# Head sums and weight spreading of a windowed attention on TensorE, with score and value steps as two streams

## The chip, the cores and the metric

One core of a Trainium2 chip. The metric is the device time of one execution, in microseconds, lower is better. Each kernel ran in alternating rounds with the kernel before, on the same chip. There were four such batches: the result, e1 to e4, e5 to e8 (both of these on chip 15), and e9 (on chip 13). Where two variants of different batches are compared, the kernel before is the link: its medians in the four batches are 1617.2, 1617.2, 1617.2 and 1617.1 us. Times of one kernel agree within about 0.2%.

Engine names as the profile writes them: PE is TensorE's matmul stream, PEld its weight loads, DVE is VectorE, ACT is ScalarE, POOL is GpSimd, SP is the engine that issues most DMAs.

## The reference

Two layers, each an attention block and a gated feed-forward block, on 2048 tokens of width 1024, bf16. Cut to what matters:

```python
def _A_ref(x, wqkv, wo):                 # 32 heads of 32 lanes
    W, dil = 8, 2                        # each token looks at itself and 7 tokens before it, 2 apart
    ...                                  # q, k, v = x @ wqkv; kg, vg = k, v at those 8 places
    logits = jnp.einsum("bhsd,bhswd->bhsw", q, kg) * scale
    logits = jnp.where(mask[None, None, :, :], logits, -1e9)
    attn = _softmax(logits, axis=-1)
    o = jnp.einsum("bhsw,bhswd->bhsd", attn, vg)
    ...                                  # @ wo

def _B_ref(x, w1, w3, w2): ...           # silu(x@w1) * (x@w3) @ w2, inner width 3584

x = x + _A_ref(_layernorm(x), ...);  x = x + _B_ref(_layernorm(x), ...)     # twice
```

The projections and the feed-forward are large matmuls. The scores and the weighted sum of values are elementwise products with short sums, because each token has its own eight keys.

## The kernel before

The program itself decides the order of the instructions on each engine: it keeps a clock of its own (`now`) for PE, VectorE and ScalarE, advances it by an expected cost for each instruction it emits, and fits attention steps into VectorE's gaps (`background`). PE and VectorE then execute strictly in that order.

The attention works on 16 pieces of 256 tokens ("halves"). Lanes are laid out so that each of the 128 partitions holds 8 of the 1024 lanes, and four neighbouring partitions make one head. So the sum over a head is a sum over 8 tiles in the same partition, which VectorE does as a tree, and then over 4 partitions, which it does with a 32x32-block transpose (arguments shortened):

```python
xnp = ctx.enter_context(tc.tile_pool(name="xn", bufs=4))     # normalised rows, waiting for their transpose
scr = ctx.enter_context(tc.tile_pool(name="scr", bufs=2))    # products of the trees
# ... cut ...
def apply(i):                                                # in norm_apply
    xn = xnp.tile([P, D], BF16, name="xn")
    nc.vector.tensor_scalar(xn[:], x_sb[:, c * TPC + j, :], mv[:, i, 0:1], rstd[:, i:i + 1], ...)
    nc.sync.dma_start_transpose(out=xnT[:, :, j * P:(j + 1) * P], in_=xn[:])
# ... cut ...
def attention_steps():
    for g, (l, h) in enumerate(halves):
        # ... cut: psm = products q*k, summed by a tree over the 8 tiles
        yield 2.35, 0.0, lambda: V.transpose(psmT, psm)           # 128x2048
        yield 2.35, 0.0, lambda: V.reduce_sum(L, psmT, axis=AX.X) # sum over 4 partitions
        # ... cut: max by three steps, subtract, exp on ScalarE, sum by three steps, reciprocal, multiply: An
        yield 1.25, 0.0, lambda: V.tensor_copy(AeT, An repeated 4 times)
        yield 2.35, 0.0, lambda: V.transpose(At, AeT)             # weights back on every lane
        # ... cut: oT = products At*v, summed by a tree
```

The output projection of a half (`o_tile`, 16 matmuls for 128 tokens, twice for a half) is placed in PE's order when the program's clock says that `oT` is ready.

Of the kernel before, what the change touches and what calls it, by code (L numbers as in the profile page):

```python
# [9 lines left out]
ALU = mybir.AluOpType  # L10
# [5 lines left out]
def kernel(  # L16
# [46 lines left out]
    PSUM, DRAM = bass.MemoryType.PSUM, bass.MemoryType.DRAM  # L63
    const = ctx.enter_context(tc.tile_pool(name="const", bufs=1))
    wp = ctx.enter_context(tc.tile_pool(name="wp", bufs=8))
    xnp = ctx.enter_context(tc.tile_pool(name="xn", bufs=4))
    xtp = ctx.enter_context(tc.tile_pool(name="xnT", bufs=2))
    scr = ctx.enter_context(tc.tile_pool(name="scr", bufs=2))
    wk = ctx.enter_context(tc.tile_pool(name="wk", bufs=1))
    smp = ctx.enter_context(tc.tile_pool(name="smp", bufs=1))  # L70
    sgp = ctx.enter_context(tc.tile_pool(name="sg", bufs=3))
# [10 lines left out]
    MM, TABLE, DMA = 0.216, 1.3, 2.5  # L82
    now = dict(pe=23.6, dve=15.0, act=24.5, table=None)
    units = [(l, c) for l in range(2) for c in range(NCH)]
    norms, attention = [], []
    x_at = [12.5, 21.5, 25.0, 28.5]
    xnT_at, norm_left, qkv_at, oT_at, o_todo = {}, {}, {}, {}, {}

# [37 lines left out]
    def background(until):  # L126

        while True:
            for queue in (norms, attention):
                s = head(queue)  # L130
                if s is not None and max(now["dve"], s[1]) + s[0] <= until:
                    take(queue)
                    break
            else:
                return
# [8 lines left out]
    def bank(name):  # L144
# [3 lines left out]
    nc.gpsimd.memset(ident[:], 0.0)  # L148
    nc.gpsimd.affine_select(out=ident[:], in_=ident[:], compare_op=ALU.not_equal, fill=1.0, base=0,
                            pattern=[[-1, P]], channel_multiplier=1)  # L150
    maskT = const.tile([P, W, 8], FP32, name="maskT")
    nc.gpsimd.memset(maskT[:], 0.0)
    for a in range(4):
        mslice = maskT[32 * a:32 * (a + 1), :, :]
        nc.gpsimd.affine_select(out=mslice, in_=mslice, compare_op=ALU.is_ge, fill=-1.0e9, base=0,
                                pattern=[[-DIL, W], [0, 8]], channel_multiplier=1)
    epst = const.tile([P, 1], FP32, name="epst")
    nc.gpsimd.memset(epst[:], EPS)

# [235 lines left out]
        qks[l, h] = qT, kT, max(now["dve"], qkv_at[l, h // R, 1]) + DMA  # L395

    def load_v(l, h):
        if (l, h) in vs or (l, h // R, 2) not in qkv_at:
            return
        vT = qkvp.tile([P, KT, HALO + TCH], BF16, name="vT")  # L400
        load_part(vT, l, 2, h * TCH, True)
        vs[l, h] = vT, max(now["dve"], qkv_at[l, h // R, 2]) + DMA

    def attention_steps():

        halves = [(l, h) for l in range(2) for h in range(NCH * R)]
        V = nc.vector
        for g, (l, h) in enumerate(halves):
            load_qk(l, h)
            while (l, h) not in qks:  # L410
                yield "blocked"
                load_qk(l, h)
            load_v(l, h)
            qT, kT, ready = qks[l, h]
            psm = wk.tile([P, W, TCH], BF16, name="psm")

            def mul_qk(w_):
                pr = scr.tile([P, KT, TCH], BF16, name="pr", tag="scr")
                k0 = HALO - DIL * w_
                V.tensor_tensor(pr[:], qT[:], kT[:, :, k0:k0 + TCH], op=ALU.mult)  # L420
                return pr

            yield 0.0, ready, lambda: None
            yield from tree(W, mul_qk, lambda w_: psm[:, w_, :])
            load_v(l, h)
            NE = TCH // 32 * 8
            psmT = smp.tile([P, W * NE, 4], BF16, name="psmT", tag="tr")
            L = smp.tile([P, W, NE], FP32, name="L", tag="L")
            m4 = smp.tile([P, 4, NE], FP32, name="m4", tag="m4")
            mx = smp.tile([P, NE], FP32, name="mx")  # L430
            E = smp.tile([P, W, NE], BF16, name="E")
            sm_ = smp.tile([P, NE], FP32, name="sm_")
            rs = smp.tile([P, NE], FP32, name="rs")
            rsb = smp.tile([P, NE], BF16, name="rsb")
            at = {}

            def exps():
                V.tensor_tensor(L[:], L[:], mx[:].unsqueeze(1).to_broadcast([P, W, NE]), op=ALU.subtract)
                nc.scalar.activation(E[:], L[:], ACTF.Exp, scale=scale)
                at["E"] = act(0.65, now["dve"] + 0.1, "exp")  # L440

            yield 2.35, 0.0, lambda: V.transpose(psmT[:].rearrange("p c d -> p (c d)"),  # L442
                                                 psm[:].rearrange("p w s -> p (w s)"))
            yield 2.35, 0.0, lambda: V.reduce_sum(L[:].rearrange("p w e -> p (w e)"), psmT[:], axis=AX.X)
            if h == 0:
                yield 0.2, 0.0, lambda: V.tensor_tensor(L[:, :, 0:8], L[:, :, 0:8], maskT[:], op=ALU.add)
            yield 0.46, 0.0, lambda: V.tensor_tensor(m4[:], L[:, 0:4, :], L[:, 4:8, :], op=ALU.max)
            yield 0.33, 0.0, lambda: V.tensor_tensor(m4[:, 0:2, :], m4[:, 0:2, :], m4[:, 2:4, :], op=ALU.max)
            yield 0.26, 0.0, lambda: V.tensor_tensor(mx[:], m4[:, 0, :], m4[:, 1, :], op=ALU.max)
            yield 0.72, 0.0, exps  # L450
            e4 = smp.tile([P, 4, NE], FP32, name="e4", tag="m4")
            An = smp.tile([P, W, NE], BF16, name="An", tag="L")
            yield 0.46, at["E"], lambda: V.tensor_tensor(e4[:], E[:, 0:4, :], E[:, 4:8, :], op=ALU.add)
            yield 0.33, 0.0, lambda: V.tensor_tensor(e4[:, 0:2, :], e4[:, 0:2, :], e4[:, 2:4, :], op=ALU.add)
            yield 0.26, 0.0, lambda: V.tensor_tensor(sm_[:], e4[:, 0, :], e4[:, 1, :], op=ALU.add)
            yield 0.60, 0.0, lambda: V.reciprocal(rs[:], sm_[:])
            yield 0.23, 0.0, lambda: V.tensor_copy(rsb[:], rs[:])
            yield 0.46, 0.0, lambda: V.tensor_tensor(An[:], E[:], rsb[:].unsqueeze(1).to_broadcast([P, W, NE]),
                                                     op=ALU.mult)
            AeT = smp.tile([P, W * NE, 4], BF16, name="AeT", tag="tr")  # L460
            At = wk.tile([P, W, TCH], BF16, name="At")
            yield 1.25, 0.0, lambda: V.tensor_copy(
                AeT[:], An[:].rearrange("p w e -> p (w e)").unsqueeze(2).to_broadcast([P, W * NE, 4]))
            yield 2.35, 0.0, lambda: V.transpose(At[:].rearrange("p w s -> p (w s)"),
                                                AeT[:].rearrange("p c d -> p (c d)"))
            if g + 1 < len(halves):
                load_qk(*halves[g + 1])
            load_v(l, h)
            while (l, h) not in vs or (g >= 2 and o_todo.get(halves[g - 2], 1)):
                yield "blocked"  # L470
                load_v(l, h)
            vT, ready = vs[l, h]
            oT = wk.tile([P, KT, TCH], BF16, name="oT", bufs=2)
            oTs[l, h] = oT

            def mul_v(t):
                tm = scr.tile([P, W, TCH], BF16, name="tm", tag="scr")
                base = vT[:, t, HALO:HALO + TCH]
                win = bass.AP(vT.tensor, base.offset, [list(base.ap[0]), [-DIL, W], [1, TCH]])
                V.tensor_tensor(tm[:], At[:], win, op=ALU.mult)  # L480
                return tm

            yield 0.0, ready, lambda: None
            yield from tree(KT, mul_v, lambda t: oT[:, t, :])
            oT_at[l, h] = now["dve"]
            o_todo[l, h] = 2

    oTs = {}
    attention.append([attention_steps(), None])

    NW = 8
    seq = [("qkv", which, h) for which in range(3) for h in range(2)]
# [46 lines left out]
    def o_tile():  # L539

        l, n = o_queue.pop(0)
        h, j = n // 2, n % 2
        force(attention, lambda: (l, h) in oT_at)
        oT = oTs[l, h]
        for hh in range(2):
            ps = bank("po")
            for t in range(KT):
                nc.tensor.matmul(ps[:], lhsT=oT[:, t, j * P:(j + 1) * P], rhs=wo[:, t, hh * 512:(hh + 1) * 512],  # L548
                                 start=(t == 0), stop=(t == KT - 1))
            r = pe(KT, oT_at[l, h] + 0.2)  # L550
            xs = x_sb[:, n, hh * 512:(hh + 1) * 512]
            background(r)
            nc.vector.tensor_tensor(xs, xs, ps[:], op=ALU.add)  # L553
            dve(0.64, r)
        o_todo[l, h] -= 1
        if j == 1:
            norm_queue.append((("B", l, n // TPC), n // TPC, (h % R,)))

    def between(hold, must=False):

        flush()
        while o_queue and (must or oT_at.get((o_queue[0][0], o_queue[0][1] // 2), 1e9) + 0.3 <= now["pe"]):
            o_tile()
            if not must:
                break
        while norm_queue and not hold:
            queue_norm(*norm_queue.pop(0))
# [181 lines left out]
```

## Time and profile before

| | before |
|---|---|
| time, median of 2 runs | 1617.2 us (1616.86 to 1617.55) |
| PE busy | 1601.8 us, 99% of the profiled span |
| VectorE busy | 1164.2 us, 72% |
| ScalarE busy | 353.2 us, 22% |
| PE waits found, in all | 2.9 us, all before 10 us |

From the page of the kernel before: the busy time of each engine with its share of the span, and, further down, the chain of waits that ended last, by engine.

```profile
PE 1601.8 (99%) x7525; PEld 805.9 (50%) x7672; DVE 1164.2 (72%) x1964; ACT 353.2 (22%) x549; POOL 1.9 (0%) x12
...
PE 94%; DVE 3%; DMA 1%; issue 1%; SPq 0%; ACT 0%; DVEq 0%
```

PE is busy nearly all the time, and the chain lies on PE. But a busy PE is not yet PE at its peak, so two more views are wanted. First the list of PE's waits (engine, line and tile that waited, who released it: us in total, times, the longest).

```profile
PE pw L168 <- DVE psm L163: 1.2, 1, 1.2
PE pT L277 <- DVE xn L268: 1.0, 1, 1.0
PE pq L286 <- DMA wqkv<-in_A_wqkv_dram: 0.7, 1, 0.7
```

Then the table by stage: length, busy time (and records) of PE, PEld, DVE, ACT, POOL, then the granted TensorE clock, the DMA share and GB/s.

```profile
40.00:100.00 60.00, 59.68 (x274) 39.88 (x279) 53.16 (x90) 21.40 (x39) 0.00 (x0) 1.00 0.52 145
100.00:200.00 100.00, 99.53 (x456) 61.32 (x464) 96.83 (x163) 32.14 (x55) 0.00 (x0) 1.00 0.72 213
```

464 weight loads in the 100 us of the second stage, one for each matmul, is one matmul of 512 columns every 216 ns, at a clock of 1.00. (Some matmul records are missing, so the loads are the better count.) The Trainium skill, "TensorE: Matmul & The Clock Gate", Part 1, section "Wait — 56ns, not 53.3ns?", has 215.7 ns measured for this size, from start to start, and the trace agrees. So the stream has no slack: whatever is added to PE must lengthen the kernel, and what is taken off VectorE can't shorten it.

The VectorE operations that the change removes, from the groups by shape (line, engine, operation, tiles, shapes, count | busy us, mean ns | idle before):

```profile
L442 DVE STREAM_TRANSPOSE psmT<-psm 128x2048 bf16<-128x2048 bf16 x16 | 36.9, 2307 | 0.2
L464 DVE STREAM_TRANSPOSE At<-AeT 128x2048 bf16<-128x2048 bf16 x16 | 36.9, 2306 | 0.1
L444 DVE TENSOR_REDUCE L<-psmT 128x512 f32<-128x2048 bf16 x16 | 36.4, 2276 | 0.1
L462 DVE COPY AeT<-An 128x2048 bf16<-128x2048 bf16 x16 | 19.6, 1225 | 0.4
```

One more view of the kernel before, which the prediction did not look at closely enough: VectorE in order of time (start, length, operation, and in brackets the idle time before it with what ended it), near the beginning.

```profile
26.62 1.00 DVE L211 TENSOR_SCALAR xn<-x_sb,mv,rstd 128x1024 bf16<-128x1024 bf16 x2
...
27.81 1.00 DVE L211 TENSOR_SCALAR xn<-x_sb,mv,rstd 128x1024 bf16<-128x1024 bf16 x2
28.73 1.28 DVE L187 BATCH_NORM_STATS2 st<-x_sb 128x6 f32<-128x512 bf16 x2
...
46.04 1.23 DVE L420 TENSOR_TENSOR pr<-qT,kT 128x2048 bf16<-128x2048 bf16 x1 [6.04 <-DMA qT<-qkv_d]
```

Four normalised tiles are written within 2.2 us, each into a buffer of its own; then VectorE goes on. It even has 6 us to spare before the first product of the scores.

### The profile page before, as it was taken

How to read it: one execution, taken by the hardware profiler on the slowest of the kernel's cores; microseconds unless marked ns; L12 is line 12 of the kernel's file. 1: busy time of each engine (PE TensorE's matmuls, PEld its weight loads, DVE VectorE, ACT ScalarE, POOL GpSimd, SP SyncE). 2: the span in 40 equal slices, each digit the busy share in tenths (PEclk: the TensorE clock that was granted, in tenths of full speed). 3: DMA queues.
4: the chain of work that ended last, by engine and by line, in shares of the span. 5: the costliest groups of instructions: out<-in, count | busy, mean ns of one | idle time of the engine just before them, and what ended most of it. 6: DMA issues, size and time to landing. Idle time of an engine off the chain costs nothing.

```text
span 1615.4 us, 19241 instructions
## 1 busy us (share of the span) xinstructions
PE 1601.8 (99%) x7525; PEld 805.9 (50%) x7672; DVE 1164.2 (72%) x1964; ACT 353.2 (22%) x549; POOL 1.9 (0%) x12
## 2 busy tenths in 40 slices
PE   9999999999999999999999999999999999999999
PEld 7665544444445544455444554445544444444444
DVE  6899998989889898997998349983599832222212
ACT  4332321212112330222302123021230212011110
POOL 0000000000000000000000000000000000000000
PEclk9999999999999999999999999999999999999999
DMA  9565955466538864478663776528675265436430
GB/s 315 138 191 164 262 166 178 131 194 182 174 105 235 249 190 145 137 211 246 159 190 121 210 236 174 190 95 262 207 223 158 94 194 169 144 109 217 156 130 27
DMA packets 336397, 285.84 MB, mean 177 GB/s; under 512 B 69681, under 2 KB 318897, under 8 KB 336177
## 3 DMA queue, kind: packets, MB, share of 16 engines
q1 hardware_dynamic: 336160, 284.46, 58.1%
q8 instruction: 60, 0.98, 0.2%
q14 instruction: 33, 0.26, 0.0%
q10 hardware_dynamic: 144, 0.13, 0.0%
HBM read 239.47 MB, written 29.36 MB: 166 GB/s over the span
## 4 chain that ended last, share of the span: by engine, by line
PE 94%; DVE 3%; DMA 1%; issue 1%; SPq 0%; ACT 0%; DVEq 0%
PE acc L653 24%; PE pu L637 23%; PE pg L629 22%; PE ps L587 19%; PE po L548 6%; PE pq L286 1%; DMA kT<-qkv_d 1%; DMA wqkv<-in_A_wqkv_dram 1%; DVE pr L420 1%; DVE pr L354 0%; DVE hT L641 0%; DVE x_sb L553 0%; DVE st L187 0%; DVE tm L354 0%; DVE tm L480 0%
## 5 line engine op out<-in xcount | busy, mean ns | idle before, releaser
L637 PE MATMUL pu<-xnT,w3t 128*128 128x512 bf16 x1763 | 420.5, 379 | 1.6
L629 PE MATMUL pg<-xnT,w1t 128*128 128x512 bf16 x1750 | 419.5, 379 | 2.1
L653 PE MATMUL acc<-w2t,hT 128*128 128x512 bf16 (+1 forms) x1768 | 387.4, 378 | 1.8
L587 PE MATMUL ps<-xnT,wqkv 128*128 128x512 bf16 x1441 | 317.6, 379 | 1.6
L633 ACT ACTIVATE sg<-pg 128x512 bf16<-128x512 f32 x224 | 133.6, 597 | 779.6 <-PE pg L629 738.9
L641 DVE TENSOR_TENSOR hT<-sg,pu 128x512 bf16<-128x512 bf16 x224 | 152.7, 682 | 191.9 <-PE pu L637 179.1
L653 PEld LDWEIGHTS <-hT 128*128 128x128 bf16 x1804 | 176.5, 98 | 210.5
L637 PEld LDWEIGHTS <-w3t 128*128 128x128 bf16 x1792 | 175.4, 98 | 211.4
L629 PEld LDWEIGHTS <-w1t 128*128 128x128 bf16 x1792 | 175.3, 98 | 211.4
L587 PEld LDWEIGHTS <-wqkv 128*128 128x128 bf16 x1472 | 211.1, 143 | 106.8
L420 DVE TENSOR_TENSOR pr<-qT,kT 128x2048 bf16<-128x2048 bf16 x128 | 155.8, 1218 | 99.5 <-DMA kT<-qkv_d 93.5
L663 DVE TENSOR_TENSOR x_sb<-x_sb,acc 128x512 bf16<-128x512 bf16 x129 | 87.3, 677 | 114.3 <-PE acc L653 109.7
L480 DVE TENSOR_TENSOR tm<-At,vT 128x2048 bf16<-128x2048 bf16 x128 | 156.0, 1219 | 0.2
L591 ACT CAST sgt<-ps 128x512 bf16<-128x512 f32 x184 | 105.1, 587 | 225.1 <-PE ps L587 183.5
L354 DVE TENSOR_TENSOR tm<-tm 128x1024 bf16<-128x1024 bf16 (+1 forms) x256 | 137.1, 552 | 0.5
L354 DVE TENSOR_TENSOR pr<-pr 128x1024 bf16<-128x1024 bf16 (+1 forms) x256 | 137.0, 551 | 0.5
L548 PE MATMUL po<-wo,oT 128*128 128x512 bf16 x503 | 115.3, 379 | 0.6
L548 PEld LDWEIGHTS <-oT 128*128 128x128 bf16 x512 | 50.1, 98 | 60.1
L187 DVE BATCH_NORM_STATS2 st<-x_sb 128x6 f32<-128x512 bf16 x120 | 75.7, 668 | 5.8 <-DMA x_sb<-in_A_x_dram 5.8
L633 ACT ACT_TABLE_LOAD x30 | 38.5, 1283 | 76.9 <-PE pg L629 76.6
L553 DVE TENSOR_TENSOR x_sb<-x_sb,po 128x512 bf16<-128x512 bf16 x64 | 43.1, 683 | 16.3 <-PE po L548 15.9
L442 DVE STREAM_TRANSPOSE psmT<-psm 128x2048 bf16<-128x2048 bf16 x16 | 36.9, 2307 | 0.2
(83 smaller groups left out, 403.7 us busy)
## 6 DMA issues: line engine op xcount, KB each, us to landing
w1t<-in_B_w_dram SPq DMA_DIRECT2D x56, 1024.0 KB, 5.5
w3t<-in_B_w_dram SPq DMA_DIRECT2D x56, 1024.0 KB, 7.8
w2t<-in_B_w_dram SPq DMA_DIRECT2D x48, 1024.0 KB, 5.7
wqkv<-in_A_wqkv_dram SPq DMA_DIRECT2D x28, 1024.0 KB, 6.8
qkv_d<-sgt SPq DMA_DIRECT2D x92, 256.0 KB, 3.3
qT<-qkv_d SPq DMA_DIRECT2D x16, 512.0 KB, 8.6
w2t<-in_B_w_dram SPq DMA_DIRECT2D x16, 512.0 KB, 5.2
kT<-qkv_d SPq DMA_DIRECT2D x14, 544.0 KB, 9.4
```

The source lines that it names most:

```text
L354: nc.vector.tensor_tensor(b[:, 0:m, :], b[:, 0:m, :], b[:, m:2 * m, :], op=ALU.add)
L420: V.tensor_tensor(pr[:], qT[:], kT[:, :, k0:k0 + TCH], op=ALU.mult)
L480: V.tensor_tensor(tm[:], At[:], win, op=ALU.mult)
L548: nc.tensor.matmul(ps[:], lhsT=oT[:, t, j * P:(j + 1) * P], rhs=wo[:, t, hh * 512:(hh + 1) * 512], start=(t == 0), stop=(t == KT - 1))
L587: nc.tensor.matmul(ps[:], lhsT=ws[kk // KH][:, kk % KH, t::KT], rhs=xnT[:, kk, :], start=(kk == 0), stop=(kk == KT - 1))
L591: nc.scalar.copy(sgt[:, t - t0, :], ps[:])
L629: nc.tensor.matmul(pg[:], lhsT=w1t[:, kk, fi * P:(fi + 1) * P], rhs=xnT[:, kk, :], start=(kk == 0), stop=(kk == KT - 1))
L633: nc.scalar.activation(sg[:], pg[:], ACTF.Silu)
L637: nc.tensor.matmul(pu[:], lhsT=w3t[:, kk, fi * P:(fi + 1) * P], rhs=xnT[:, kk, :], start=(kk == 0), stop=(kk == KT - 1))
L641: nc.vector.tensor_tensor(hT[:, f - f0, :], sg[:], pu[:], op=ALU.mult)
L653: nc.tensor.matmul(acc[:], lhsT=hT[:, f - f0, j * P:(j + 1) * P], rhs=w2ts[(f - f0) // 8][:, (f - f0) % 8, q0:q0 + step], start=(f == f0), ...
L663: nc.vector.tensor_tensor(xs, xs, acc[:], op=ALU.add)
```

## The change

The intent: take the transposes, the sum over four partitions and the fourfold copy off VectorE. The sum over the four partitions of a head becomes a matmul with a 0/1 matrix `gather` (128 by 32), one for each quarter of the tokens, put on its own 32 output partitions. The spread of the weights back over the lanes becomes a matmul with a 0/1 matrix `spread` (128 by 128), copied out of PSUM by ScalarE. The generator of attention steps is cut into two, scores and values, so that one can go on while the other waits for PE. Requests for PE are queued and emitted between groups of matmuls, one at a time, when the program's clock says that the input is there. To make room, one `xn` buffer is given for a third `scr` buffer.

```diff
-    xnp = ctx.enter_context(tc.tile_pool(name="xn", bufs=4))
+    xnp = ctx.enter_context(tc.tile_pool(name="xn", bufs=3))
-    scr = ctx.enter_context(tc.tile_pool(name="scr", bufs=2))
+    scr = ctx.enter_context(tc.tile_pool(name="scr", bufs=3))
@@ background @@
-            for queue in (norms, attention):
+            for queue in (norms, values, scores):
@@ constants: gather and spread are built on GpSimd; cut @@
+    def pe_requests(limit=1, must=False):
+        while pe_queue and limit and (must or pe_queue[0][0] + 0.3 <= now["pe"]):
+            pe_queue.pop(0)[1]()
+            limit -= 1
@@ score_steps, after the tree @@
-            yield 2.35, 0.0, lambda: V.transpose(psmT..., psm...)
-            yield 2.35, 0.0, lambda: V.reduce_sum(L..., psmT[:], axis=AX.X)
+            def gather_heads(t):
+                at["L"] = L = psum.tile([P, W, BLK], FP32, name="L", tag="mm")
+                for a in range(4):
+                    nc.tensor.matmul(L[32 * a:32 * (a + 1), :, :], lhsT=gather[:],
+                                     rhs=psm[:, :, a * BLK:(a + 1) * BLK], start=True, stop=True)
+                at["t"] = pe(3, t) + 0.2
+            t = now["dve"] + 0.2
+            pe_queue.append((t, lambda: gather_heads(t)))
@@ max and sum: one tensor_reduce each in place of three steps each; cut @@
-            yield 1.25, 0.0, lambda: V.tensor_copy(AeT..., An... 4 times)
-            yield 2.35, 0.0, lambda: V.transpose(At..., AeT...)
+            def spread_heads(a):
+                ps = psum.tile([P, W, BLK], FP32, name="pe", tag="mm")
+                nc.tensor.matmul(ps[:], lhsT=spread[:, a, :], rhs=An[:], start=True, stop=True)
+                r = pe(1, t2)
+                nc.scalar.copy(At[:, :, a * BLK:(a + 1) * BLK], ps[:])
@@ value_steps: the tree of the values as before, in a generator of its own; cut @@
@@ between: called after each group of matmuls @@
         flush()
+        pe_requests()
```

More of the change, by code (lines that the diff above doesn't have):

```diff
@@ L84 @@
     units = [(l, c) for l in range(2) for c in range(NCH)]
-    norms, attention = [], []
+    norms = []
     x_at = [12.5, 21.5, 25.0, 28.5]
@@ L150 @@
                             pattern=[[-1, P]], channel_multiplier=1)
-    maskT = const.tile([P, W, 8], FP32, name="maskT")
+    maskT = const.tile([32, W, HALO], FP32, name="maskT")
     nc.gpsimd.memset(maskT[:], 0.0)
-    for a in range(4):
-        mslice = maskT[32 * a:32 * (a + 1), :, :]
-        nc.gpsimd.affine_select(out=mslice, in_=mslice, compare_op=ALU.is_ge, fill=-1.0e9, base=0,
-                                pattern=[[-DIL, W], [0, 8]], channel_multiplier=1)
+    nc.gpsimd.affine_select(out=maskT[:], in_=maskT[:], compare_op=ALU.is_ge, fill=-1.0e9, base=0,
+                            pattern=[[-DIL, W], [1, HALO]], channel_multiplier=0)
+    gather = const.tile([P, 32], BF16, name="gather")
+    spread = const.tile([P, 4, P], BF16, name="spread")
+    for t, pattern, base, slope in ((gather, [[-4, 32]], 0, 1), (spread, [[P, 4], [1, P]], 0, -4)):
+        nc.gpsimd.memset(t[:], 1.0)
+        nc.gpsimd.affine_select(out=t[:], in_=t[:], compare_op=ALU.is_ge, fill=0.0, base=base,
+                                pattern=pattern, channel_multiplier=slope)
+        nc.gpsimd.affine_select(out=t[:], in_=t[:], compare_op=ALU.is_ge, fill=0.0, base=3 - base,
+                                pattern=[[-st, n] for st, n in pattern], channel_multiplier=-slope)
     epst = const.tile([P, 1], FP32, name="epst")
@@ L397, in load_v @@
     def load_v(l, h):
-        if (l, h) in vs or (l, h // R, 2) not in qkv_at:
+        if (l, h) in vs or (l, h // R, 2) not in qkv_at or len(av_done) < len(vs):
             return
@@ L402, in load_v, with score_steps @@
         vs[l, h] = vT, max(now["dve"], qkv_at[l, h // R, 2]) + DMA
-    def attention_steps():
-        halves = [(l, h) for l in range(2) for h in range(NCH * R)]
+    pe_queue = []
+    L_at, At_at, Ats, av_done = {}, {}, {}, set()
+    halves = [(l, h) for l in range(2) for h in range(NCH * R)]
+    BLK = TCH // 4
+    def pe_requests(limit=1, must=False):
+        while pe_queue and limit and (must or pe_queue[0][0] + 0.3 <= now["pe"]):
+            pe_queue.pop(0)[1]()
+            limit -= 1
+    def score_steps():
         V = nc.vector
@@ L425, in attention_steps @@
             load_v(l, h)
-            NE = TCH // 32 * 8
-            psmT = smp.tile([P, W * NE, 4], BF16, name="psmT", tag="tr")
-            L = smp.tile([P, W, NE], FP32, name="L", tag="L")
-            m4 = smp.tile([P, 4, NE], FP32, name="m4", tag="m4")
-            mx = smp.tile([P, NE], FP32, name="mx")
-            E = smp.tile([P, W, NE], BF16, name="E")
-            sm_ = smp.tile([P, NE], FP32, name="sm_")
-            rs = smp.tile([P, NE], FP32, name="rs")
-            rsb = smp.tile([P, NE], BF16, name="rsb")
@@ L435, in attention_steps @@
-            at = {}
-            def exps():
-                V.tensor_tensor(L[:], L[:], mx[:].unsqueeze(1).to_broadcast([P, W, NE]), op=ALU.subtract)
-                nc.scalar.activation(E[:], L[:], ACTF.Exp, scale=scale)
-                at["E"] = act(0.65, now["dve"] + 0.1, "exp")
-            yield 2.35, 0.0, lambda: V.transpose(psmT[:].rearrange("p c d -> p (c d)"),
-                                                 psm[:].rearrange("p w s -> p (w s)"))
-            yield 2.35, 0.0, lambda: V.reduce_sum(L[:].rearrange("p w e -> p (w e)"), psmT[:], axis=AX.X)
@@ L445, in attention_steps @@
-            if h == 0:
-                yield 0.2, 0.0, lambda: V.tensor_tensor(L[:, :, 0:8], L[:, :, 0:8], maskT[:], op=ALU.add)
-            yield 0.46, 0.0, lambda: V.tensor_tensor(m4[:], L[:, 0:4, :], L[:, 4:8, :], op=ALU.max)
-            yield 0.33, 0.0, lambda: V.tensor_tensor(m4[:, 0:2, :], m4[:, 0:2, :], m4[:, 2:4, :], op=ALU.max)
-            yield 0.26, 0.0, lambda: V.tensor_tensor(mx[:], m4[:, 0, :], m4[:, 1, :], op=ALU.max)
-            yield 0.72, 0.0, exps
-            e4 = smp.tile([P, 4, NE], FP32, name="e4", tag="m4")
@@ L452, in attention_steps @@
-            An = smp.tile([P, W, NE], BF16, name="An", tag="L")
-            yield 0.46, at["E"], lambda: V.tensor_tensor(e4[:], E[:, 0:4, :], E[:, 4:8, :], op=ALU.add)
-            yield 0.33, 0.0, lambda: V.tensor_tensor(e4[:, 0:2, :], e4[:, 0:2, :], e4[:, 2:4, :], op=ALU.add)
-            yield 0.26, 0.0, lambda: V.tensor_tensor(sm_[:], e4[:, 0, :], e4[:, 1, :], op=ALU.add)
-            yield 0.60, 0.0, lambda: V.reciprocal(rs[:], sm_[:])
-            yield 0.23, 0.0, lambda: V.tensor_copy(rsb[:], rs[:])
@@ L458, in attention_steps @@
-            yield 0.46, 0.0, lambda: V.tensor_tensor(An[:], E[:], rsb[:].unsqueeze(1).to_broadcast([P, W, NE]),
-                                                     op=ALU.mult)
-            AeT = smp.tile([P, W * NE, 4], BF16, name="AeT", tag="tr")
-            At = wk.tile([P, W, TCH], BF16, name="At")
-            yield 1.25, 0.0, lambda: V.tensor_copy(
-                AeT[:], An[:].rearrange("p w e -> p (w e)").unsqueeze(2).to_broadcast([P, W * NE, 4]))
-            yield 2.35, 0.0, lambda: V.transpose(At[:].rearrange("p w s -> p (w s)"),
-                                                AeT[:].rearrange("p c d -> p (c d)"))
@@ L466, in attention_steps @@
             if g + 1 < len(halves):
                 load_qk(*halves[g + 1])
+            at = {}
+            def gather_heads(t):
[5 more added lines that the diff above has]
+            t = now["dve"] + 0.2
@@ new lines, in score_steps @@
+            pe_queue.append((t, lambda: gather_heads(t)))
+            while "t" not in at:
+                yield "blocked"
+            L = at["L"]
+            Ls = smp.tile([P, W, BLK], FP32, name="Ls")
+            mx = smp.tile([P, BLK], FP32, name="mx")
+            E = smp.tile([P, W, BLK], BF16, name="E")
+            sm_ = smp.tile([P, BLK], FP32, name="sm_")
+            rs = smp.tile([P, BLK], FP32, name="rs")
+            An = smp.tile([P, W, BLK], BF16, name="An")
+            yield 0.0, at["t"], lambda: None
@@ new lines, in score_steps, with exps @@
+            if h == 0:
+                yield 0.2, 0.0, lambda: V.tensor_tensor(L[0:32, :, 0:HALO], L[0:32, :, 0:HALO], maskT[:],
+                                                        op=ALU.add)
+            yield 0.68, 0.0, lambda: V.tensor_reduce(mx[:], L[:].rearrange("p w e -> p e w"), op=ALU.max, axis=AX.X)
+            def exps():
+                V.tensor_tensor(Ls[:], L[:], mx[:].unsqueeze(1).to_broadcast([P, W, BLK]), op=ALU.subtract)
+                nc.scalar.activation(E[:], Ls[:], ACTF.Exp, scale=scale)
+                at["E"] = act(0.65, now["dve"] + 0.1, "exp")
@@ new lines, in score_steps @@
+            yield 0.70, 0.0, exps
+            yield 0.0, at["E"] if "E" in at else 0.0, lambda: None
+            yield 0.66, at["E"], lambda: V.tensor_reduce(sm_[:], E[:].rearrange("p w e -> p e w"), op=ALU.add,
+                                                         axis=AX.X)
+            yield 0.56, 0.0, lambda: V.reciprocal(rs[:], sm_[:])
+            yield 0.68, 0.0, lambda: V.tensor_tensor(An[:], E[:], rs[:].unsqueeze(1).to_broadcast([P, W, BLK]),
+                                                     op=ALU.mult)
@@ new lines, in score_steps @@
+            while g >= 1 and halves[g - 1] not in av_done:
+                yield "blocked"
+            At = Ats[l, h] = wk.tile([P, W, TCH], BF16, name="At")
+            t2 = now["dve"] + 0.2
+            def spread_heads(a):
[3 more added lines that the diff above has]
+                nc.scalar.copy(At[:, :, a * BLK:(a + 1) * BLK], ps[:])
+                done = act(0.6, r)
+                if a == 3:
+                    At_at[l, h] = done
@@ L468, in attention_steps, with value_steps @@
+            for a in range(4):
+                pe_queue.append((t2, lambda a=a: spread_heads(a)))
+            while (l, h) not in At_at:
+                yield "blocked"
+    def value_steps():
+        V = nc.vector
+        for g, (l, h) in enumerate(halves):
+            while (l, h) not in At_at or (g >= 2 and o_todo.get(halves[g - 2], 1)):
+                yield "blocked"
             load_v(l, h)
-            while (l, h) not in vs or (g >= 2 and o_todo.get(halves[g - 2], 1)):
+            while (l, h) not in vs:
@@ L470, in attention_steps @@
                 yield "blocked"
                 load_v(l, h)
+            At = Ats[l, h]
             vT, ready = vs[l, h]
@@ L481, in mul_v @@
                 return tm
-            yield 0.0, ready, lambda: None
+            yield 0.0, max(ready, At_at[l, h]), lambda: None
             yield from tree(KT, mul_v, lambda t: oT[:, t, :])
@@ L486, in attention_steps @@
             o_todo[l, h] = 2
+            av_done.add((l, h))
+            if g + 1 < len(halves):
+                load_v(*halves[g + 1])
     oTs = {}
-    attention.append([attention_steps(), None])
+    values, scores = [[value_steps(), None]], [[score_steps(), None]]
     NW = 8
@@ L542, in o_tile @@
         h, j = n // 2, n % 2
-        force(attention, lambda: (l, h) in oT_at)
+        while (l, h) not in oT_at:
+            for queue in (values, scores):
+                if head(queue) is not None:
+                    take(queue)
+                    break
+            else:
+                assert pe_queue
+                pe_requests(1, True)
         oT = oTs[l, h]
```

## The prediction

> **What bounds the kernel now.** TensorE. The page's busy table gives PE 1601.8 us of a 1615.4 us span (99%), the chain that ended last is 94% PE, the granted clock is 1.00. The table by stage shows 99.5 us of PE in every 100 us from 100 to 1600 us, with 463 to 464 weight loads: one 128x512 matmul per 216 ns. (The groups' "mean 379 ns" includes latency that the next matmul overlaps.) The list of PE's waits holds three entries, 2.9 us together, all in the first 10 us. The Trainium skill ("TensorE: Matmul & The Clock Gate", Back-to-back issue gap; measured 215.7 ns for N=512) agrees with this trace: the stream has no idle time to win.
>
> VectorE is 72% busy (1164 us), but PE never waits for it after the start: it is off the critical path.
>
> **What the change removes.** Per half-chunk of attention (16 in all), from the groups by shape: two 128x2048 stream transposes (2.31 us each), the sum over four (2.28), the fourfold copy (1.22), the small max and sum ladders, subtract, reciprocal, casts: about 190 us of VectorE in all.
>
> **What it adds.** VectorE: five operations per half of 0.55 to 0.7 us, some 53 us; so 1164 falls to about 1030 us. ScalarE: 64 evictions at 0.59 us, so 353 rises to about 391. TensorE, in the built order: exactly 128 more matmuls and weight loads, nothing else:
> - 64 spread matmuls, full array, 512 columns: 64 x 0.216 = 13.8 us.
> - 64 gather matmuls of 32 output columns, in 16 groups of four. The skill (same page, Part 3) says matmuls on different 32-column strips run side by side (2.38x for three). Then four cost about 0.3 us, and entering and leaving should expose the neighbours' latency, 379 - 216 = 0.16 us an end: about 0.65 us a group, 10 us in all (estimate). One after another they would take 0.86 + 0.3 us a group, 19 us.
>
> **What moves.** Values come ahead of scores in VectorE's background; gathers and spreads are slipped between PE groups when the program expects their inputs ready. In the built order each projection stands over 100 matmuls (24 us) behind the last spread of its half, so I expect no long wait: 0 to 4 us in total over 32 hand-overs. One scratch buffer more and one xn buffer fewer do nothing; the longer setup on GpSimd costs under 0.5 us.
>
> **Sum.** All PE additions are on the critical path, all VectorE savings off it: 1617 + 13.8 + 10 + 1 = 1642 us, 1.5% slower. Range 1635 to 1650. Faster by over 2%: 1%. Within 2%: 87%. Slower by over 2%: 12%.
>
> **What would show each step.** PE still 99% busy with no idle in the middle, its busy time up by the same 20 to 30 us as the span; spread matmuls spaced by 216 ns; a gather group taking about 0.65 us between its neighbours; VectorE near 1030 us and ScalarE near 391 without effect; PE's waits on VectorE's products and weights under 4 us.
>
> **What would make it wrong.** (a) Gathers serialise, or draining costs more than 0.16 us an end: toward 1650 or above. (b) Inputs of gathers and spreads come later than the program expects, so that PE, in order, stalls a microsecond at each of 32 places: 1650 to 1675. (c) ScalarE, waiting in order for a spread, holds back a gate activation until PSUM buffers run out: PE idle released by ScalarE. (d) Gathers overlap fully: 1635.

## The result, and the profile after

| | before | after |
|---|---|---|
| time, median of 2 runs | 1617.2 us | 1666.4 us |
| ratio after/before | | 1.030 (95% interval 1.027 to 1.033) |
| PE busy | 1601.8 us | 1631.1 us |
| VectorE busy | 1164.2 us | 1042.5 us |
| ScalarE busy | 353.2 us | 387.7 us |
| mean granted clock | 1.000 | 0.993 |

A ratio is the mean time of one kernel's fast runs over that of the other's of the same rounds, so it is not quite the ratio of the medians quoted. The changed kernel is 49.2 us slower, outside the predicted range of 1635 to 1650 us.

The page of the changed kernel, busy times and chain:

```profile
PE 1631.1 (98%) x7650; PEld 813.6 (49%) x7800; DVE 1042.5 (63%) x1820; ACT 387.7 (23%) x611; POOL 3.2 (0%) x15
...
PE 91%; DVE 5%; DMA 3%; issue 1%; SPq 0%; ACT 0%; DVEq 0%
```

There are 128 weight loads more, as predicted, and VectorE lost its 122 us. But 3% of the chain now lies on DMA and 5% on VectorE. PE's waits show it:

```profile
PE L L449 <- DVE psm L362: 9.2, 3, 6.8
PE L L449 <- DVE vT L389: 7.0, 1, 7.0
PE pe L489 <- DVE An L480: 4.3, 2, 4.0
```

20.5 us of PE stalls, 17.8 of them three long ones: two before a gather and one before a spread. (The matmul of the line put down to `vT` reads `psm`, whose last piece was written just before, from 68.47 to 68.76 us.) The table by stage says where, and shows a second effect: the clock.

```profile
40.00:100.00 60.00, 48.82 (x202) 29.09 (x205) 36.75 (x71) 21.90 (x43) 0.00 (x0) 0.86 0.44 124
100.00:200.00 100.00, 92.76 (x417) 58.01 (x424) 70.09 (x125) 31.52 (x54) 0.00 (x0) 0.97 0.58 165
```

Between 40 and 200 us PE lost about 18 us of busy time, and worked at 0.86 and 0.97 of its clock. PE in order of time:

```profile
68.91 0.62 PE L449 MATMUL L<-psm,gather 128*32 128x512 bf16 x4 [6.97 <-DVE vT L389]
69.46 9.52 PE L638 MATMUL ps<-xnT,wqkv 128*128 128x512 bf16 x31
82.98 0.59 PE L489 MATMUL pe<-An,spread 128*128 128x512 bf16 x1 [4.00 <-DVE An L480]
83.36 5.94 PE L638 MATMUL ps<-xnT,wqkv 128*128 128x512 bf16 x16
...
145.12 0.62 PE L449 MATMUL L<-psm,gather 128*32 128x512 bf16 x4 [6.82 <-DVE psm L362]
145.67 8.97 PE L638 MATMUL ps<-xnT,wqkv 128*128 128x512 bf16 x32
...
1062.94 27.79 PE L704 MATMUL acc<-w2t,hT 128*128 128x512 bf16 x126
1090.66 0.40 PE L449 MATMUL L<-psm,gather 128*32 128x512 bf16 x4
1091.00 1.90 PE L680 MATMUL pg<-xnT,w1t 128*128 128x512 bf16 x8
```

After each stall the matmuls are slow for a while: the 32 after the first gather (one record is missing) take 9.5 us, where 31 x 0.216 us and the 0.38 us of the last one, 7.1 us, would do; the next 16, from 83.36 to the next spread at 89.14, take 5.8 us in place of 3.5; the 32 after the second late gather take 8.8 us, up to the spread at 154.48, in place of 6.9. Together 2.4 + 2.3 + 1.9 = 6.6 us. (The first 2.4 us are hidden: at full clock PE would only have waited longer for the spread's input.) The Trainium skill, "TensorE: Matmul & The Clock Gate", Part 1, says that the clock is halved when PE has been idle for a window of about 3.4 us, and comes back after a busy window. For these stalls this trace agrees: the granted clock is 0.50 from 69 to 74 us and from 83 to 88 us, and 1.00 again after. (Shorter stalls are in the list at the end.)

The last three lines are an undisturbed gather. From the start of the last full matmul before it to the first gather are 309 ns in the trace's own time stamps, from there to the next full matmul 332 ns; nearly all undisturbed groups of this kernel and of e5 agree within 2 ns. Without gathers it would be 216 ns from one full matmul to the next. So four gathers cost PE 309 + 332 - 216 = 425 ns, 0.43 us, less than the predicted 0.65 us. (Some expectations below use 0.44, a first reading of this place.)

Why is VectorE late? VectorE in order of time:

```profile
27.36 1.00 DVE L217 TENSOR_SCALAR xn<-x_sb,mv,rstd 128x1024 bf16<-128x1024 bf16 x2
...
28.55 0.55 DVE L217 TENSOR_SCALAR xn<-x_sb,mv,rstd 128x1024 bf16<-128x1024 bf16 x1
38.62 0.55 DVE L217 TENSOR_SCALAR xn<-x_sb,mv,rstd 128x1024 bf16<-128x1024 bf16 x1 [9.52 <-DMA xnT<-xn]
...
50.27 1.18 DVE L436 TENSOR_TENSOR pr<-qT,kT 128x2048 bf16<-128x2048 bf16 x1
...
80.06 0.55 DVE L217 TENSOR_SCALAR xn<-x_sb,mv,rstd 128x1024 bf16<-128x1024 bf16 x1 [6.88 <-DMA xnT<-xn]
```

There are three `xn` buffers, and a chunk has four tiles. The fourth must wait until the transposing DMA of the first has read its buffer: 9.5 us. At this time the DMAs are full (two weight tiles of 1 MB were queued just before; the DMA share between 20 and 40 us is 1.01), and that transpose lands 8.9 us after its issue, where the median is 3.5 us. VectorE executes in order, so everything after it waits too. The first product of the scores starts at 50.27 us, 4.2 us later than before. The same wait comes again at 73 to 80 us (6.9 us) and at 126 to 134 us (8.0 us), each time between VectorE's steps that a gather or spread depends on, and each time PE stalls behind it. The wait at 126 us is like the first (8.3 us from issue to landing). The one at 73 us is not: there the transposes land 3.2 to 3.4 us after their issue, but SP, which issues in order too, comes to the first of them only at 76.66 us, 4.6 us after its rows were written. Before it stands a store that waits for ScalarE's copy of a late output of PE. So the second wait is in part an effect of PE's first stall.

The sum of what the trace shows: spreads 64 x 0.216 = 13.8 us, gathers 16 x 0.425 = 6.8 us, the three long stalls 17.8 us, slow matmuls 6.6 us, later stalls 2.7 us: 48 of 49 us. Whether the stalls come from the `xn` buffer or from the hand-overs themselves is a matter of experiment.

### The profile page after: what moved, and what is told of

It is laid out like the page before. It is cut to its first block, busy times and chain, and to the rows that moved or that the text cites. A ratio compares the mean times of both kernels' runs of the same rounds, so it can differ in the third digit from the quotient of the medians.

```text
span 1664.7 us, 19422 instructions
## 1 busy us (share of the span) xinstructions
PE 1631.1 (98%) x7650; PEld 813.6 (49%) x7800; DVE 1042.5 (63%) x1820; ACT 387.7 (23%) x611; POOL 3.2 (0%) x15
## 4 chain that ended last, share of the span: by engine, by line
PE 91%; DVE 5%; DMA 3%; issue 1%; SPq 0%; ACT 0%; DVEq 0%
PE acc L704 23%; PE pu L688 23%; PE pg L680 22%; PE ps L638 16%; PE po L598 6%; DVE pr L436 1%; DMA xnT<-xn 1%; DVE pr L360 1%; DMA x_sb<-in_A_x_dram 1%; DVE st L193 1%; PE pe L489 1%; DMA kT<-qkv_d 1%; PE L L449 0%; DVE x_sb L603 0%; DVE psm L362 0%
## 5 line engine op out<-in xcount | busy, mean ns | idle before, releaser
L638 PE MATMUL ps<-xnT,wqkv 128*128 128x512 bf16 x1442 | 327.2, 385 | 1.6
L491 ACT CAST At<-pe 128x512 bf16<-128x512 f32 x64 | 37.4, 587 | 75.6 <-PE pe L489 75.6
L217 DVE TENSOR_SCALAR xn<-x_sb,mv,rstd 128x1024 bf16<-128x1024 bf16 x60 | 30.8, 544 | 32.1 <-DMA xnT<-xn 30.8
```

The lines of the kernel that those rows point to most:

```text
L638: nc.tensor.matmul(ps[:], lhsT=ws[kk // KH][:, kk % KH, t::KT], rhs=xnT[:, kk, :], start=(kk == 0), stop=(kk == KT - 1))
```

## The experiments

The theory: the fourth `xn` buffer is the cause of the long stalls ("buffer theory"). The rival: the round trips PE, VectorE, ScalarE, PE come later than the program's clock expects, whatever the buffers ("round trips"). A first trial with four `xn` and three `scr` buffers could not be built: the last pool needs 12.5 KB per partition and 11.4 were left. So the exchange of one for the other was forced by room, and each had to be tested apart.

### e1: the fourth buffer back

```diff
-    xnp = ctx.enter_context(tc.tile_pool(name="xn", bufs=3))
+    xnp = ctx.enter_context(tc.tile_pool(name="xn", bufs=4))
-    scr = ctx.enter_context(tc.tile_pool(name="scr", bufs=3))
+    scr = ctx.enter_context(tc.tile_pool(name="scr", bufs=2))
```

> The changed kernel with its fourth xn buffer back (and scr at two again, for room); instruction order on every engine unchanged. Buffer theory: the 9.5, 6.9 and 8.0 us waits of VectorE for a free xn go, with them PE's stalls at 69, 83 and 145 us (17.8 us) and the lowered clock after them (about 7 us): 1641 us, 1638 to 1646. Rival (the round trips TensorE-VectorE-ScalarE themselves come later than the program expects): the stalls stay, 1658 or more.

Measured: 1647.3 us (ratio to before 1.0185, 1.017 to 1.020); 19.1 us came back, and in the traces VectorE, ScalarE and PE's weight loads have the same instructions in the same order as in the changed kernel. VectorE in order of time, at the place of the 9.5 us wait:

```profile
28.15 1.01 DVE L217 TENSOR_SCALAR xn<-x_sb,mv,rstd 128x1024 bf16<-128x1024 bf16 x2
29.07 1.28 DVE L193 BATCH_NORM_STATS2 st<-x_sb 128x6 f32<-128x512 bf16 x2
```

The list of PE's waits of e1, without its short ones:

```profile
PE L L449 <- DVE vT L389: 3.2, 1, 3.2
PE L L449 <- DVE psm L362: 2.3, 1, 2.3
```

The buffer theory holds for the larger part: of 20.5 us of stalls 5.8 are left. It had promised 1641 us, though, and the range was missed by 1.3 us: the first gather still waits 3.2 us (with some matmuls at the lowered clock after it: 32 take 8.65 us in place of 6.9), and one in the second layer 2.3 us (the 16 matmuls after it take 5.15 us in place of 3.45). Here the rival is right on a small scale.

### e2: is it scr?

The changed kernel with `scr` at two and `xn` left at three.

> The changed kernel with scr at two and xn left at three: is it scr or xn? Buffer theory: scr does nothing, so 1666 within 2 us and the same stalls. If the third scr buffer were worth something, slower than 1668.

Measured: 1666.1 us, the same as the changed kernel, with the same stalls (7.4, 7.2 and 3.9 us the longest). The third `scr` buffer is worth nothing; e1 differs from e2 in `xn` alone, so the whole gain of e1, 18.7 us in the same rounds, belongs to `xn`.

### e3: the same buffer taken from the kernel before

```diff
-    xnp = ctx.enter_context(tc.tile_pool(name="xn", bufs=4))
+    xnp = ctx.enter_context(tc.tile_pool(name="xn", bufs=3))
```

> The kernel before with three xn buffers instead of four, nothing else. Buffer theory: VectorE shows the same waits for xn in the first 150 us (20 us or more), and PE, whose first output projections stand near 185 us, waits for them: 1622 to 1645. Rival (round trips): 1617 within 2 us.

Measured: 1625.5 us, 8.3 us slower than before, inside the range. VectorE waits 21.2 us for `xn`, but only 14.8 us of it in the first 150 us, less than the 20 us expected there, and the path to PE was not the expected one. VectorE near the beginning:

```profile
28.84 0.55 DVE L211 TENSOR_SCALAR xn<-x_sb,mv,rstd 128x1024 bf16<-128x1024 bf16 x1
38.79 0.55 DVE L211 TENSOR_SCALAR xn<-x_sb,mv,rstd 128x1024 bf16<-128x1024 bf16 x1 [9.41 <-DMA xnT<-xn]
```

And all engines near 135 us (lines of other engines left out):

```profile
135.01 0.63 ACT L439 ACTIVATE E<-L 128x512 bf16<-128x512 f32 x1 [13.23 <-DVE L L438]
135.55 3.00 ACT L591 CAST sgt<-ps 128x512 bf16<-128x512 f32 x6
...
136.17 9.17 PE L587 MATMUL ps<-xnT,wqkv 128*128 128x512 bf16 x32 [5.03 <-ACT sgt L591]
```

The projections wait only 0.6 us. Instead ScalarE, which works in order too, stands 13 us before an exponential whose input is late; behind it stand the copies that free PSUM, and PE runs out of banks for 5.0 us, then works at the lowered clock (32 matmuls recorded in 9.2 us). So the buffer costs the old kernel 8 us and the new one 19. Two differences stand beside this number, and no run separates them: in the new one PE itself waits for VectorE's intermediate results, not only for the finished output; and its waits for `xn` in the first 150 us were longer, 24.4 us against 14.8.

### e4: the two streams alone

The stream split kept; head sums and spread back on VectorE as in the kernel before; `xn` four, `scr` two.

> The two streams alone: head sums and spread back on VectorE as before, xn four, scr two; PE instructions as many as before. Both theories: the split into streams is neutral, 1617 within 3 us, no PE wait over 1 us after the start. If the reordering itself makes PE wait: 1625 or more.

Measured: 1617.55 us, ratio 1.0002 (0.9987 to 1.0017). The reordering is neutral, and VectorE at 1165.1 us busy costs nothing: the 122 us that the change takes off VectorE buy no time.

### e5: asking later for the gathers

On top of e1:

```diff
-            pe_queue.append((t, lambda: gather_heads(t)))
+            pe_queue.append((t + (3.5 if g == 0 else 2.5 * l), lambda: gather_heads(t)))
```

> As e1, and the program asks for the gathers a little later than it did: 3.5 us for the first, 2.5 us for those of the second layer. If the 5.8 us of stalls left in e1 are hand-overs that come a few us too early, they go: PE waits under 1 us after the start, the clock at 1.00, and what is left is TensorE work, 64 x 0.216 = 13.8 us of spreads and 16 x 0.44 = 7 us of gathers: 1638 us, 1636 to 1641. If the stalls only move: 1645 or more.

Measured: 1642.4 us (1641.8 to 1644.2), with the clock at 1.000 in three of four runs; the slowest has 0.999. The longest of PE's waits (the projections wait 0.7 us, and the start 2.5 us):

```profile
PE pe L489 <- DVE An L480: 2.3, 1, 2.3
```

The gathers no longer wait, 4.9 us came back, but 2.3 us moved to the first spread, so the range was missed by 1.4 us. By the spans of the profiles the kernel is now 24.7 us over before (1640.1 against 1615.4): 13.8 + 6.8 + 3.0 of stalls explains 23.6.

### e6, e7, e8: what the added matmuls cost

All three on top of e5, with the same order otherwise.

```diff
 e6   -  nc.tensor.matmul(ps[:], lhsT=spread[:, a, :], rhs=An[:], ...)
      +  for _ in range(2): nc.tensor.matmul(ps[:], lhsT=spread[:, a, :], rhs=An[:], ...)
 e7   -  for a in range(4):                        # gathers
      +  for a in (0, 1, 2, 3, 0, 1, 2, 3):
 e8   -  nc.tensor.matmul(L[32 * a:32 * (a + 1), :, :], lhsT=gather[:], rhs=..., start=True, stop=True)
      +  nc.tensor.matmul(L[:], lhsT=gather4[:, a, :], rhs=..., start=(a == 0), stop=(a == 3))
```

> As e5, each spread matmul issued twice in a row (the same result): 64 more full matmuls. If a spread costs its 216 ns of stream and nothing hides it: 13.8 us over e5, 12.5 to 15. If spreads also cost something for entering and leaving, it does not show here; if TensorE had idle time for them, under 10.

> As e5, each group of four gather matmuls issued twice in a row (the same result): 64 more matmuls of 32 columns. Side by side on four column strips: 16 x 0.216 = 3.5 us over e5, 2.5 to 5. One after another: 13.8 us, 12 to 15.

> As e5, the gather without column strips: four matmuls over the full array that accumulate into one bank, each with its 32 columns of the stationary operand filled and the rest zero (the same result). Strips side by side (0.44 us a group): this takes 4 x 0.216 = 0.86 us a group, so 6 to 8 us over e5. If the strips gained nothing over plain matmuls: within 1.5 us of e5.

Measured, against e5's 1642.4 us: e6 1657.4 us (+14.9), e7 1647.3 us (+4.8), e8 1648.6 us (+6.2). All three lie in their ranges. A gather group of e7 and one of e8, PE in order of time:

```profile
372.67 1.89 PE L688 MATMUL pu<-xnT,w3t 128*128 128x512 bf16 x8
374.49 0.62 PE L449 MATMUL L<-psm,gather 128*32 128x512 bf16 x8
375.03 1.90 PE L680 MATMUL pg<-xnT,w1t 128*128 128x512 bf16 x8
```

```profile
370.89 1.89 PE L692 MATMUL pu<-xnT,w3t 128*128 128x512 bf16 x8
372.62 1.03 PE L453 MATMUL L<-psm,gather 128*128 128x512 bf16 x4
373.48 1.89 PE L684 MATMUL pg<-xnT,w1t 128*128 128x512 bf16 x8
```

From the first gather to the next full matmul, in the trace's time stamps: 332 ns for four on column strips (e5 and the changed kernel), 548 ns for eight (e7), 863 ns for four over the full array (e8). So four more gathers on strips cost 216 ns, the time of one full matmul, and the four of a group start 3 to 4 ns apart: they do run side by side.

A part of the measured differences is the clock. After the stall of 2.4 us that e7's first spread has, 16 matmuls take 4.84 us in place of 3.45, at a clock of 0.57; after e5's stall of 2.3 us they do not. So e7's +4.8 us is 16 x 0.216 = 3.5 us of gathers and about 1.4 us of slow matmuls, and all four of its runs have a mean clock of 0.999. Of e6's four runs three have 0.999 too. The one at 1.000 took 1655.9 us, against 1642.0 us, the median of e5's three at 1.000: 13.9 us for 64 spreads, or 0.217 us each, their full place in the stream.

### e9: the stalls filled

To tell the stalls from the lowered clock: the changed kernel as it is, with useless matmuls of constants put where PE would fall idle.

```diff
+            def fill(n):
+                pw = bank("pw")
+                for _ in range(n):
+                    nc.tensor.matmul(pw[:], lhsT=ident[:], rhs=spread..., start=True, stop=True)
             def gather_heads(t):
+                if g < 2: fill(30)
             def spread_heads(a):
+                if g == 0 and a == 0: fill(28)
```

> The changed kernel as it is (xn three), with 30, 28 and 30 useless full matmuls put in where PE stalls for 7.0, 4.0 (6.8 at full clock) and 6.8 us, so that PE does not fall idle. The inputs it waits for come at the same times. If the lowered clock after the stalls costs time of its own: the clock of the stages 40 to 200 us goes back to about 1.00, and 2.3 us (16 matmuls after the first spread) and 1.9 us (32 after the second gather) come back: 1662 us, 1660 to 1664. If the clock costs nothing: 1666 or, with fill that is too long, more.

Measured: 1661.6 us (1660.6 to 1663.0), 88 matmuls more and 4.8 us less than the changed kernel. The table by stage of e9:

```profile
40.00:100.00 60.00, 58.98 (x276) 36.06 (x275) 40.09 (x77) 22.88 (x45) 0.00 (x0) 1.00 0.47 131
100.00:200.00 100.00, 100.00 (x467) 61.73 (x466) 70.62 (x126) 30.22 (x53) 0.00 (x0) 1.00 0.61 180
```

The clock is back at 1.00. The lowered clock after the stalls thus cost about 4 to 5 us of the 49, apart from the stalls themselves. A busy PE in this table would look perfect, although 19 us of its work (88 x 0.216) is worthless: a reminder that busy time is not useful time.

## Why the prediction was wrong

- "All PE additions are on the critical path, all VectorE savings off it": right. VectorE fell by 122 us, and e4, with all of VectorE's work back, ran in 1617.55 us.
- The 64 spread matmuls, 13.8 us: right in size. Doubling them cost 13.9 us in runs of the same clock (14.9 us by the medians).
- The 16 groups of four gathers, about 0.65 us each, 10 us: the mechanism was right, the size too high. A group takes 0.43 us, 6.8 us in all; I had charged 0.16 us of exposed latency at each end, and the measured overhead of both ends together is 425 - 216 = 209 ns, about 0.21 us. That is 3 us in the other direction from the miss.
- "VectorE near 1030 us and ScalarE near 391 without effect": 1042.5 and 387.7 us.
- **"One scratch buffer more and one xn buffer fewer do nothing" is the step that failed.** Half of the sentence is right (e2: the scratch buffer does nothing). The `xn` buffer made VectorE wait 30.8 us in eight places, up to 9.5 us at once, and giving it back (e1) returned 19.1 us of the 49.2, to 1647.3 us, inside the predicted range. The evidence lay in the profile before: four `xn` tiles written in 2.2 us, then held by DMAs that took up to 9.1 us to land. I counted buffers without asking what holds them, and for how long, at the moment when all four are wanted.
- "No long wait: 0 to 4 us in total over 32 hand-overs": wrong with it, 20.5 us. With the buffer restored it was 5.8 us (e1), over the predicted 4; so this term failed mostly through the buffer, and for a smaller part by itself. That e1 is nevertheless inside the range has luck in it: the gathers, 3 us cheaper than predicted, make up for a part of it.
- The alternative (b) named late inputs, "a microsecond at each of 32 places". The time it gave, 1650 to 1675 us, holds the result, but its shape was wrong: three stalls of 4 to 7 us, all in the first 150 us, behind VectorE's waits for one buffer (3.2 us of the first stay in e1).
- Not in the prediction at all: a stall of several us lowers PE's clock, which by e9 cost another 4 to 5 us.

In e1 and e5 the parts (spreads, gathers, stalls, slow matmuls) explain 0.5 to 1 us less than the difference of the profiled spans to before; where that is, stays open. That full DMAs hold the `xn` buffer is read from the traces; no run moved the weight loads away to test it. No version tried beats the kernel before: e4 equals it, and every spread or gather on a PE that already runs at 216 ns per matmul adds its own time. The best version with both matmuls, e5, is 1.6% slower than before.

## What to carry to other kernels

Move work onto an engine only if that engine has time: on a stream that is already at its issue rate, each added full-array matmul costs its full length, and time freed on another engine buys nothing. Before giving up a buffer, find in the trace the place where all of its siblings are in use at once, and how long their readers hold them, the time in the queue that issues the readers included; an in-order engine turns one missing buffer into a delay of everything after it. And where the bounding engine consumes intermediate results of another, the other's delays, harmless until then, become stalls, which here also lowered the clock for some microseconds after.

## What the Trainium skill lacked or had wrong

- "TensorE: Matmul & The Clock Gate", Part 2, section "Back-to-back issue gap", gives about 131 ns as the sustained time of a 512-column matmul in a stream with weight loads, and calls 216 ns too high for it. Here such a stream ran at 216 ns: 464 weight loads in 100 us, at a clock of 1.00.
- "TensorE: Matmul & The Clock Gate", Part 3, measures three matmuls on column strips (2.38x) but not four, nor the cost of a short group inside a stream of full-array matmuls. Here four of 512 columns took 0.43 us of the stream in all, against 0.86 us over the full array, and four more only 0.22 us.
- "TensorEngine Tiling (Array Packing)", Key Properties, says that changing the tiling mode drains the array, without a number. Here entering and leaving cost 0.21 us together.
- "TensorE: Matmul & The Clock Gate", Part 1, on the lowered clock after an idle window of about 3.4 us: agreed for the stalls of 7.0, 4.0 and 6.8 us, where the loss was 2.4, 2.3 and 1.9 us. But shorter stalls were followed by it as well: 3.2 and 2.3 us (e1, losses of 1.75 and 1.7 us) and 2.4 us (e7, 1.4 us). Stalls of 2.2 us (changed kernel, second layer), 2.3 us (e5) and 2.5 us (e6) were not, in the profiled runs. What decides between these, no run here shows.
- No page that I read says how long a transposing DMA holds its source tile when the DMA engines are full. Here a 128x1024 tile took 3.1 to 9.0 us to land, median 3.5 us, and the missing buffer made VectorE wait up to 9.5 us.
